# Fused attention and two MLPs on one core: phase one's small group at its end, and conversion work at other steps

## The chip, the cores and the metric

One core of one Trainium2 chip runs the whole program. The metric is device time in microseconds (us) of one execution; the median of several is compared. Nothing is shared with other cores.

## The reference

```python
I = inducing                                   # 32 x 128
h = softmax(I @ x.T / sqrt(128)) @ x           # over 12480 tokens: 32 x 128
x1 = softmax(x @ h.T / sqrt(128)) @ h          # 12480 x 128
g = max(x1 @ w_in, 0) + alpha * min(x1 @ w_in, 0)   # 12480 x 2048
x2 = g @ w_out                                 # 12480 x 128
out = max(x2 @ w2_in, 0) ** 2 @ w2_out         # 12480 x 128
```

x and inducing are fp32; the four weight matrices (128x2048 or 2048x128) and alpha come in 8-byte words, so a quarter of a weight matrix is 512 KB and is turned into fp32 on the chip.

## The kernel before, in words

All large products run in a reduced fp32 format, each operand split into a high and a low part; `three` (L688 to 691) does hi*hi, lo*hi and hi*lo into one PSUM bank. There are eight PSUM banks: h1 (two), h2 (two), y1 (one), y2 (two), ms (one). The order on every engine is the order in which the program issues the instructions; nothing is reordered.

**Phase one** (L359 to 456) reads x in groups of four sub-tiles: first a small group of 4x48 tokens, then six of 4x512. For group g the loop does `scores(g)`, the values of the group before (`values1`), running maximum and exp (`maxima`, `exps`), the transposes of the next group's x (`transpose_x`, four banks, two copies by ScalarE, two by VectorE), and the transposes of e (`transpose_e`). Between these stand the conversions of w_in and w_out (`to_f32`, L181 to 210), each with five parts: MAG and LOW on ScalarE, BITS and SIGN on VectorE, ADD on GpSimd; a w_out quarter also has REST (GpSimd), HI (ScalarE) and LO (GpSimd). MAG writes a PSUM bank where one is given, else SBUF. Behind the loop (L402 to 456) come the last group, the weights `wgt` by which the four row groups of 32 are joined, the matrix `sel`, the denominator, and hT, the result of the first attention.

**Start of the main part** (L618 to 644). The softmax of the first 512 tokens (`first_attention`), the product w1 of hT and w_in (`make_w1`, `make_first_w1s`, `copy_w1`, `low_w1`), and the DMAs on SyncE that lay w1's parts into w1s (`spread_w1s`). With w1s a tile's first layer is one matmul on its attention weights a_s.

**Main loop** (L816 to 830). 25 tiles (21 of 512 tokens, three of 448, one of 384) times 16 chunks of the hidden width give 400 items. In step s PE does `l1_a(s)` (first layer, then g1h on ScalarE and g1l on VectorE), `l2_a(s-24)`, `l1_b` of an item three to five steps back and `l2_b(s-28)`; l2_split, one step after l2_a, makes g2h on ScalarE and g2l on GpSimd. So the first steps hold 1 to 4 large matmuls and all steps from 28 on 10. Two lists hang other work on steps: `at(...)` (L783 to 804) for the second softmax (`second_attention`: tiles 1 to 4 first, whose seven parts end in 16 DMAs into a_s) and for v, and PIECES (L254 to 259), whose tuples give the steps of MAG, LOW, BITS, SIGN, ADD and split for the eight quarters of w2_in and w2_out; a quarter's buffer is freed by its ADD, and then the load of the quarter four places on is issued on SyncE's queue. Tile 1 begins with l1_a(16).

```python
at(5, second[3])
at(6, second[4])
at(9, second[5])
at(10, second[6])
```

The last tile's rows are copied, transposed and written by two engines in parallel (`last_rows`, L759 to 774).

Of the kernel before, what the change touches and what calls it, by code (L numbers as in the profile page):

```python
# [30 lines left out]
def attention_then_two_mlps(ctx: ExitStack, tc, x, inducing, w_in, w_out, alpha, w2_in, w2_out, out):  # L31
# [108 lines left out]
    def load_x(g, part=None):  # L140
        _, n, p, r = groups1[g][0]
        if g in x_t:
            t = x_t[g]
# [6 lines left out]
        k = (Q, 1, 2)[min(g, 2)]  # L150
        for a in range(0, len(groups1[g]), k) if part is None else [k * part]:
            t0, kk = groups1[g][a][0], min(k, len(groups1[g]))
            (nc.scalar if g == 1 and a % 2 else nc.sync).dma_start(
                out=t[:p, a : a + kk, :r],
                in_=x[0, t0 : t0 + kk * n, :].rearrange("(t p r) c -> p t r c", p=p, r=r),
            )
# [138 lines left out]
    def scores(g):  # L295
        b = ms_bank()
# [73 lines left out]
    idle_bank = y2_bank()  # L370
    keep_busy(1, idle_bank)
    for g in range(last):
        if g:
            run(convs[g - 1][:2])
# [13 lines left out]
        if g:
            run(convs[g - 1][3:5])
        if 1 < g and g + XBUFS - 1 <= last:  # L390
            load_x(g + XBUFS - 1)
        if 0 < g <= 4:
            load_w("w_out", g - 1)
        if g == 2:
# [7 lines left out]
    b = scores(last)  # L402
    values1(last - 1)
# [3 lines left out]
    maxima(last, b)  # L407
    exps(last, b)
# [5 lines left out]
    transpose_e(last)  # L414
# [17 lines left out]
    nc.vector.tensor_scalar(sel, same, wgt, None, op0=ALU.mult)  # L432
# [32 lines left out]
    def first_attention():  # L465
# [41 lines left out]
        def step_split():
            d = a_s[0] = new_a_s(0)[: 3 * M]
            nc.scalar.copy(d, v["b"][: 3 * M, : wide[0]])
            lo = d[M : 2 * M]  # L510
            nc.vector.tensor_tensor(lo, v["b"][M : 2 * M, : wide[0]], f32(lo), op=ALU.subtract)

        return [step_scores, step_max, step_exp, step_sum, step_back, step_split]
# [347 lines left out]
```

## Time and profile before

| | us |
|---|---|
| median of 3 runs (lowest, highest) | 962.77 (961.51, 962.86) |
| profiled execution | 961.23 |
| its span, first to last instruction | 959.4 |
| PE busy | 949.3 (99%) |
| ScalarE, VectorE, GpSimd busy | 727.4, 649.9, 536.9 |

The busy share of PE counts matmuls from issue to modelled end, and they overlap; 99% therefore hides places where the pace falls. Matmuls of 512 columns that follow one another start about 0.23 us apart. In the rows further down PE is TensorE, PEld its weight loads, ACT is ScalarE, DVE is VectorE, POOL is GpSimd, SP is SyncE, and a trailing q is an engine's issuing queue.

### The profile page before, as it was taken

The numbers are of one execution on the slowest core, as the hardware profiler recorded it, in microseconds if no ns is written. First come the engines' busy times: TensorE is split into PE (matmuls) and PEld (weight loads), VectorE is DVE, ScalarE is ACT, GpSimd is POOL, SyncE is SP. The second block draws the span as 40 slices with busy tenths as digits, with TensorE's granted clock in tenths as the row PEclk, the third lists the DMA queues.
The fourth block names the chain that finished last, engine by engine and source line by source line (L and its number), as shares of the span: only waits on it lengthen the run. The fifth ranks groups of instructions, "written<-read, shape, count | busy, mean of one in ns | idle before, by whom it ended". The sixth has DMA issues, their size and how long they took to land.

```text
span 959.4 us, 13675 instructions
## 1 busy us (share of the span) xinstructions
PE 949.3 (99%) x4560; PEld 787.6 (82%) x4560; DVE 649.9 (68%) x1013; ACT 727.4 (76%) x1333; POOL 536.9 (56%) x435
## 2 busy tenths in 40 slices
PE   9989999999999999999999999999999999999998
PEld 7667778888878888878888878888888888899997
DVE  5788767666667766667666667766666766666677
ACT  5779777777777777777777777777777777777776
POOL 2548755655555655555665555565555665555530
PEclk9999999999999999999999999999999999999999
DMA  9542000020000020000020000020000020000000
GB/s 343 163 111 82 1 12 12 9 47 12 1 12 12 3 52 12 1 12 12 1 55 12 1 12 1 12 55 1 12 12 1 12 48 1 12 12 4 8 11 19
DMA packets 64551, 29.00 MB, mean 30 GB/s; under 512 B 52208, under 2 KB 57440, under 8 KB 64480
## 3 DMA queue, kind: packets, MB, share of 16 engines
q1 hardware_dynamic: 64000, 27.52, 11.5%
q8 instruction: 36, 0.59, 0.3%
q10 hardware_dynamic: 480, 0.61, 0.2%
q14 instruction: 35, 0.29, 0.1%
HBM read 14.80 MB, written 6.39 MB: 22 GB/s over the span
## 4 chain that ended last, share of the span: by engine, by line
PE 89%; ACT 2%; DVE 1%; issue 1%; POOL 0%; POOLq 0%; DVEq 0%
PE y L691 17%; PE y L690 17%; PE y L689 17%; PE h L689 9%; PE h L690 9%; PE h L691 9%; PE h L679 8%; PE y L707 1%; PE ms L524 1%; ACT g1h L683 0%; ACT r L723 0%; DVE mag L199 0%; ACT g2h L732 0%; ACT raw L195 0%; DVE mag L205 0%
## 5 line engine op out<-in xcount | busy, mean ns | idle before, releaser
L734 POOL TENSOR_TENSOR g2l<-sq,g2h 128x512 fp32r<-128x512 f32 (+1 forms) x376 | 480.0, 1278 | 342.6 <-ACT g2h L732 331.6
L685 DVE SCALAR_TENSOR_TENSOR g1l<-h,g1h 128x512 fp32r<-128x512 f32 (+2 forms) x400 | 270.0, 677 | 230.3 <-ACT g1h L683 225.1
L683 ACT ACTIVATE g1h<-h 128x512 fp32r<-128x512 f32 (+2 forms) x400 | 234.2, 588 | 141.9 <-PE h L679 140.7
L725 DVE TENSOR_TENSOR sq<-h,r 128x512 f32<-128x512 f32 (+2 forms) x400 | 271.1, 678 | 53.9 <-ACT r L723 16.9
L723 ACT ACTIVATE r<-h 128x512 f32<-128x512 f32 (+2 forms) x400 | 235.8, 589 | 61.2 <-PE h L691 16.8
L732 ACT CAST g2h<-sq 128x512 fp32r<-128x512 f32 (+2 forms) x400 | 240.8, 602 | 2.6 <-DVE sq L725 2.6
L679 PE MATMUL h<-a_s,w1s 128*128 128x512 f32 (+3 forms) x400 | 155.0, 389 | 2.8 <-DMA a_s<-a_lo 1.4
L689 PE MATMUL h<-y1h,w2i_hi 128*128 128x512 f32 (+2 forms) x400 | 154.3, 386 | 0.3
L690 PE MATMUL y<-g2h,w2o_lo 128*128 128x512 f32 (+2 forms) x400 | 153.8, 385 | 0.0
L691 PE MATMUL h<-y1l,w2i_hi 128*128 128x512 f32 (+2 forms) x400 | 153.8, 384 | 0.0
L690 PE MATMUL h<-y1h,w2i_lo 128*128 128x512 f32 (+2 forms) x400 | 153.7, 384 | 0.0
L691 PE MATMUL y<-g2l,w2o_hi 128*128 128x512 f32 (+2 forms) x400 | 153.7, 384 | 0.0
L689 PE MATMUL y<-g2h,w2o_hi 128*128 128x512 f32 (+2 forms) x400 | 153.7, 384 | 0.0
L691 PE MATMUL y<-g1l,wo_hi 128*128 128x512 f32 (+2 forms) x400 | 153.7, 384 | 0.0
L690 PE MATMUL y<-g1h,wo_lo 128*128 128x512 f32 (+2 forms) x400 | 153.7, 384 | 0.0
L689 PE MATMUL y<-g1h,wo_hi 128*128 128x512 f32 (+2 forms) x400 | 153.7, 384 | 0.0
L679 PEld LDWEIGHTS h<-a_s,w1s 128*128 128x128 f32 (+1 forms) x400 | 75.0, 188 | 25.3 <-DVE sq L725 4.1
L689 PEld LDWEIGHTS h<-y1h,w2i_hi 128*128 128x128 f32 x400 | 75.1, 188 | 16.1 <-DVE sq L725 1.8
L690 PEld LDWEIGHTS y<-g1h,wo_lo 128*128 128x128 f32 x400 | 75.1, 188 | 14.8
L689 PEld LDWEIGHTS y<-g1h,wo_hi 128*128 128x128 f32 x400 | 75.1, 188 | 14.3
L691 PEld LDWEIGHTS y<-g2l,w2o_hi 128*128 128x128 f32 x400 | 75.1, 188 | 14.2 <-DVE g2l L734 0.3
L691 PEld LDWEIGHTS y<-g1l,wo_hi 128*128 128x128 f32 x400 | 75.1, 188 | 13.9
(156 smaller groups left out, 664.5 us busy)
## 6 DMA issues: line engine op xcount, KB each, us to landing
out_dram<-o SPq DMA_DIRECT2D x84, 64.0 KB, 2.0
xg<-in_x_dram SPq DMA_DIRECT2D x8, 512.0 KB, 9.1
raw<-in_moe_w_in_dram SPq DMA_DIRECT2D x8, 512.0 KB, 5.7
raw<-in_moe_w_out_dram SPq DMA_DIRECT2D x8, 512.0 KB, 4.6
a_s<-a_hi SPq DMA_DIRECT2D x40, 64.0 KB, 2.0
a_s<-a_lo SPq DMA_DIRECT2D x40, 64.0 KB, 2.0
x_last<-in_x_dram SPq DMA_DIRECT2D x2, 512.0 KB, 9.9
out_dram<-o SPq DMA_DIRECT2D x12, 56.0 KB, 1.9
```

Source lines behind the costliest of these rows:

```text
L524: nc.tensor.matmul(b[i * M : (i + 1) * M, :w], hT[:, :M], xT[:, first_token[t + 1] - w : first_token[t + 1]], start=True, stop=True, tile_ ...
L679: nc.tensor.matmul(b[:, :w], w1s[: a.shape[0], c * P : (c + 1) * P], a, start=True, stop=True)
L683: nc.scalar.activation(hi, b[:, :w], AF.Relu)
L685: nc.vector.scalar_tensor_tensor(lo, b[:, :w], 0.0, f32(hi), op0=ALU.max, op1=ALU.subtract)
L689: nc.tensor.matmul(b, w_hi, hi, start=start, stop=False)
L690: nc.tensor.matmul(b, w_lo, hi, start=False, stop=False)
L691: nc.tensor.matmul(b, w_hi, lo, start=False, stop=stop)
L707: nc.tensor.matmul(b, v_s[: a.shape[0]], a, start=False, stop=True)
L723: nc.scalar.activation(r, b, AF.Relu)
L725: nc.vector.tensor_tensor(sq, b, r, op=ALU.mult)
L732: nc.scalar.copy(hi, sq)
L734: (nc.vector if i >= total - LAG2 else nc.gpsimd).tensor_tensor(lo, sq, f32(hi), op=ALU.subtract)
```

## The change

Phase one starts with a wide group, and the small one comes last, its transposes in the step of the last wide group's and its scores, exp and values behind that group's. The loads are issued in another order and not interleaved in halves. The matrix sel is made by ScalarE. In the first softmax, the product, the transposes and the split go in two halves; the low part of w1s' first 512 columns too, and w1l is made by GpSimd. The last w_out quarter is converted ahead of the main loop (MAG in an h1 bank) but for HI and LO. The second softmax of tiles 1 to 4 has its exp at step 8 instead of 5, sum at 9 instead of 6, way back at 12 instead of 9, split and DMAs at 13 instead of 10; v's three parts stand at 9, 10 and 12 instead of 11, 13 and 16. The w2 quarters' steps differ, and the last has its MAG in the ms bank. l1_a uses h2 for even and h1 for odd steps up to 23 and h1 from then on, where it was the other way round up to 23. The last rows are copied in pieces of 128 columns and cut at 256 instead of 128.

```diff
-    groups1 = [[(i * n0, *FIRST1) for i in range(Q)]]
+    groups1 = []
     for a in range(Q * n0, N, Q * TILE1[0]):
         groups1.append([(a + i * TILE1[0], *TILE1) for i in range(Q)])
+    groups1.append([(i * n0, *LAST1) for i in range(Q)])
+    last = len(groups1) - 1
...
-    keep_busy(4, idle_bank)
+    keep_busy(5, idle_bank)
...
-        return to_f32("w_out", k, lambda: f, h2_bank if k == 2 else None) + [rest, high, low]
+        return to_f32("w_out", k, lambda: f, {2: h2_bank, 3: h1_bank}.get(k)) + [rest, high, low]
...
-        ("w2_in", 0, y2_bank, (12, 13, 14, 14, 14, 18)), ("w2_in", 1, y2_bank, (16, 17, 18, 18, 18, 21)),
-        ("w2_out", 0, ms_bank, (19, 20, 21, 21, 21, 24)), ("w2_in", 2, ms_bank, (23, 23, 24, 24, 24, 27)),
-        ("w2_out", 1, y1_bank, (25, 25, 26, 26, 26, 29)), ("w2_in", 3, ms_bank, (27, 28, 28, 28, 28, 31)),
-        ("w2_out", 2, y1_bank, (30, 30, 31, 31, 31, 34)), ("w2_out", 3, None, (33, 33, 34, 34, 34, 38)),
+        ("w2_in", 0, y2_bank, (8, 9, 10, 11, 11, 15)), ("w2_in", 1, y2_bank, (15, 16, 17, 18, 18, 21)),
+        ("w2_out", 0, ms_bank, (19, 20, 21, 22, 22, 25)), ("w2_in", 2, ms_bank, (23, 24, 24, 25, 25, 28)),
+        ("w2_out", 1, y1_bank, (25, 26, 26, 27, 27, 30)), ("w2_in", 3, ms_bank, (27, 28, 28, 29, 29, 32)),
+        ("w2_out", 2, y1_bank, (29, 30, 30, 31, 31, 34)), ("w2_out", 3, ms_bank, (31, 32, 32, 33, 33, 36)),
...
+    nc.scalar.dma_start(out=ind, in_=inducing)
     load_x(0)
+    load_w("w_in", 0)
     load_x(1)
-    load_x(2, 0)
-    load_w("w_in", 0)
-    load_x(2, 1)
-    load_x(3, 0)
     load_w("w_in", 1)
-    load_x(3, 1)
+    load_x(2)
     nc.sync.dma_start(out=al_raw, in_=alpha.rearrange("(c p) -> c p", p=P))
+    load_w("w_in", 2)
+    load_x(3)
+    load_w("w_in", 3)
     load_x(4)
-    load_w("w_in", 2)
-    load_x(5)
-    load_w("w_in", 3)
+    load_x(last)
...
         run(transpose_x(g + 1))
+        if g == last - 2:
+            run(transpose_x(last))
         transpose_e(g)
...
-    nc.vector.tensor_scalar(sel, same, wgt, None, op0=ALU.mult)
+    nc.scalar.mul(sel, same, wgt)
+    values1(last - 1)
     values1(last)
...
     convs[6][SIGN]()
+    convs[7][BITS]()
     convs[5][REST]()
...
     def low_w1():
-        nc.vector.tensor_tensor(w1["lo"], w1["bank"], f32(w1["hi"]), op=ALU.subtract)
+        pool_lo(w1["lo"], w1["f"], w1["hi"])
...
     copy_w1()
     first[3]()
+    run(mult)
     low_w1()
-    first[4]()
-    first_w1s_low()
-    first[5]()
+    run(back)
+    run(high)
+    first_w1s_low(0, 256)
+    run(low)
+    first_w1s_low(256, 512)
+    convs[7][SIGN]()
+    convs[7][ADD]()
     step_wa()
     convs[5][HI]()
     convs[6][HI]()
+    convs[7][REST]()
...
     spread_w1s("lo", 3)
+    load_w(*PIECES[3][:2])
     convs[5][LO]()
...
-        b = h2_bank() if other_bank else h1_bank()
+        b = h1_bank() if other_bank else h2_bank()
...
-        cut = w // P // 2 * P
+        cut = w - P
...
-    at(5, second[3])
-    at(5, convs[7][BITS])
-    at(6, second[4])
-    at(7, convs[7][SIGN])
-    at(7, convs[7][ADD])
-    at(7, load_w, *PIECES[3][:2])
-    at(9, second[5])
-    at(10, second[6])
-    at(10, convs[7][REST])
-    at(11, step_v)
-    at(13, copy_v)
-    at(13, convs[7][HI])
-    at(13, convs[7][LO])
-    at(16, split_v)
+    at(6, convs[7][HI])
+    at(6, convs[7][LO])
+    at(8, second[3])
+    at(9, second[4])
+    at(9, step_v)
+    at(10, copy_v)
+    at(12, second[5])
+    at(12, split_v)
+    at(13, second[6])
...
-            l1_a(s, s < LAG2 and s % 2)
+            l1_a(s, s >= LAG2 or s % 2)
```

## Rows read from the trace of the kernel before

**Rows 1.** Busy time by stretches: stretch; then us busy and instructions of each engine
```profile
200.00:900.00 700.00, 700.00 (x3137) 582.68 (x3136) 460.99 (x684) 532.60 (x953) 403.77 (x317) 1.00 0.07 14
```

**Rows 2.** Timeline, PE, first transposes: start, us from start to end, engine, line
```profile
5.75 3.65 PE L286 MATMUL h<-ident,xg 128*128 128x128 f32 x16
...
11.40 1.97 PE L286 MATMUL h<-ident,xg 128*128 128x128 f32 x16
```

**Rows 3.** DMA issues by line: count, size, median us to landing
```profile
xg<-in_x_dram SPq DMA_DIRECT2D x2, 256.0 KB, 4.8
```

**Rows 4.** Timeline, PE and ScalarE, last group's transposes of x and e
```profile
31.25 0.64 PE L339 MATMUL y<-ident,e 128*128 128x128 f32 x4
...
31.45 0.59 ACT L289 COPY xT<-h 128x512 f32<-128x512 f32 x1 [0.35 <-PE h L286]
```

**Rows 5.** Timeline: the small group's exp, and the end of phase one
```profile
5.76 0.30 ACT L323 ACTIVATE e<-ms,nm 128x48 f32<-128x48 f32 x1 [1.64 <-DVE nm L318]
...
37.25 1.29 POOL L208 TENSOR_TENSOR w_out_sb<-mag,raw 128x512 int32<-128x512 int32 x1 [2.08 <-ACT raw L195]
37.27 1.35 DVE L432 TENSOR_SCALAR sel<-same,wgt 128x128 f32<-128x128 f32 x1
...
39.80 0.29 DVE L448 TENSOR_TENSOR hT<-y,den 128x128 f32<-128x128 f32 x1
```

**Rows 6.** Timeline, DVE and PE, from the first softmax to the first l1_a
```profile
43.03 0.56 DVE L495 TENSOR_TENSOR a<-y,mx 128x384 f32<-128x384 f32 x1
...
43.51 0.68 DVE L598 TENSOR_TENSOR w1l<-h,w1h 128x512 fp32r<-128x512 f32 x1
...
45.00 0.68 DVE L511 TENSOR_TENSOR a_s<-y,a_s 32x512 fp32r<-32x512 f32 x1
...
45.74 1.19 PE L679 MATMUL h<-a_s,w1s 96*128 96x512 f32 x4
```

**Rows 7.** DVE, groups from 46.85 to 57.3 us, and its last row there
```profile
L685 DVE SCALAR_TENSOR_TENSOR g1l<-h,g1h 128x512 fp32r<-128x512 f32 x10 | 6.5, 672 | 1.2 <-ACT g1h L683 1.2
L205 DVE SCALAR_TENSOR_TENSOR mag<-raw,mag 128x512 int32<-128x512 int32 x1 | 1.3, 1278 | 0.0
...
57.26 0.69 DVE L554 STREAM_TRANSPOSE a2t<-a 128x512 f32<-128x512 f32 x1
```

**Rows 8.** Timeline, SyncE's queue and PE up to l1_a(16); the wait's busy times
```profile
57.54 0.34 SPq L178 DMA_DIRECT2D raw<-in_moe_w_in_dram  x1
...
61.20 0.58 SPq L565 DMA_DIRECT2D a_s<-a_lo  x1
...
63.33 0.47 PE L679 MATMUL h<-a_s,w1s 128*128 128x512 f32 x1 [1.41 <-DMA a_s<-a_lo]
...
61.90:63.30 1.40, 0.03 (x1) 0.00 (x0) 0.59 (x1) 1.27 (x3) 1.09 (x1) 1.00 0.50 117
```

**Rows 9.** Timeline, POOL, first and last of 19 operations from 75.77 to 100.71
```profile
75.77 1.29 POOL L213 TENSOR_TENSOR w2o_lo<-wf,w2o_hi 128x512 fp32r<-128x512 f32 x1 [1.44 <-ACT w2o_hi L247]
...
99.39 1.32 POOL L213 TENSOR_TENSOR w2o_lo<-wf,w2o_hi 128x512 fp32r<-128x512 f32 x1
```

**Rows 10.** Timeline, DVE and PE, the last w2 quarter's BITS and PE behind it
```profile
98.20 2.79 DVE L199 TENSOR_SCALAR mag<-mag 128x512 int32<-128x512 int32 x1
...
100.77 0.50 PE L690 MATMUL y<-g2h,w2o_lo 128*128 128x512 f32 x1
...
102.97 0.50 PE L689 MATMUL h<-y1h,w2i_hi 128*128 128x512 f32 x1
```

**Rows 11.** Timeline of the tail; then the granted clock (third from right) behind it
```profile
955.00 0.27 ACT L765 COPY o<-y 128x128 f32<-128x128 f32 x1 [1.12 <-PE y L691]
...
955.32 0.90 PE L769 MATMUL h<-ident,o 128*128 128x128 f32 x3 [0.36 <-ACT o L765]
...
956.25 0.42 DVE L771 COPY r<-h 128x256 f32<-128x256 f32 x1 [0.53 <-PE h L769]
...
958.40:959.40 1.00, 0.00 (x0) 0.00 (x0) 0.00 (x0) 0.00 (x0) 0.00 (x0) 0.50 0.00 0
```

More of the change, by code (lines that the diff above doesn't have):

```diff
@@ L149, in load_x @@
             t = st.tile([n, Q, r, C], F32, name="x0", tag="x0")
[L150 to L155, printed above, removed]
-            )
-            if g == 0:
-                nc.scalar.dma_start(out=ind, in_=inducing)
+        k = Q if g == last else 2 if g else 1
+        for a in range(0, Q, k) if part is None else [k * part]:
+            t0 = groups1[g][a][0]
+            (nc.scalar if g == 0 and a % 2 else nc.sync).dma_start(
+                out=t[:p, a : a + k, :r],
+                in_=x[0, t0 : t0 + k * n, :].rearrange("(t p r) c -> p t r c", p=p, r=r),
+            )
         x_t[g] = t
@@ L293, in transpose_x, with scores @@
         return evac
-    def scores(g):
-        b = ms_bank()
+    def scores(g, bank=ms_bank):
+        b = bank()
         for i, (t0, n, _, _) in enumerate(groups1[g]):
@@ L305, in attention_then_two_mlps @@
     nm, e, f, s_g, eT, hb = {}, {}, {}, {}, {}, {}
-    last = len(groups1) - 1
     def small(name):
-        return att.tile([P, 1], F32, name=name, tag=name, bufs=2)
+        return att.tile([P, 1], F32, name=name, tag=name, bufs=3 if name == "f" else 2)
     def maxima(g, b):
@@ L332, in sums, with transpose_e @@
             nc.vector.tensor_copy(s_run, s_g[g])
-    def transpose_e(g):
+    def transpose_e(g, bank=y1_bank):
         _, _, p, r = groups1[g][0]
-        b = y1_bank()
+        b = bank()
         own = e[g].rearrange("n (p r) -> n r p", r=r)
@@ L369, in attention_then_two_mlps @@
     nc.vector.tensor_copy(indT, b[:, :M])
[L370 to L374, printed above, removed]
+    run(transpose_x(0))
+    for g in range(last - 1):
+        run(convs[g][:2])
         b = scores(g)
@@ L383, in attention_then_two_mlps @@
             add_values(g - 1)
-            convs[g - 1][2]()
+        convs[g][2]()
         run(transpose_x(g + 1))
+        if g == last - 2:
+            run(transpose_x(last))
         transpose_e(g)
         sums(g)
[L388 to L394, printed above, removed]
+        run(convs[g][3:5])
+        if g == 1:
+            load_x(XBUFS)
+        if g < 4:
+            load_w("w_out", g)
+        if g == 1:
             b = y2_bank()
@@ L400, in attention_then_two_mlps @@
     MAG, LOW, BITS, SIGN, ADD, REST, HI, LO = range(8)
-    b = scores(last)
-    values1(last - 1)
+    b, bs = scores(last - 1), scores(last, h1_bank)
+    values1(last - 2)
     convs[4][REST]()
@@ L406, in attention_then_two_mlps @@
     convs[6][MAG]()
-    maxima(last, b)
-    exps(last, b)
+    maxima(last - 1, b)
+    maxima(last, bs)
+    exps(last - 1, b)
+    exps(last, bs)
     b = y2_bank()
@@ L413, in attention_then_two_mlps @@
     convs[4][HI]()
-    transpose_e(last)
+    transpose_e(last - 1)
+    transpose_e(last, h2_bank)
     m_all = att.tile([1, M], F32, name="m_all", tag="m_all")
@@ L421, in attention_then_two_mlps @@
     keep_busy(2, idle_bank)
-    add_values(last - 1)
+    add_values(last - 2)
+    sums(last - 1)
     sums(last)
-    nnm = att.tile([P, 73 + M], F32, name="nnm", tag="nnm")[:, :1]
+    nnm = att.tile([P, 65 + M], F32, name="nnm", tag="nnm")[:, :1]
     nc.vector.tensor_scalar_mul(nnm, nm[last], -1.0)
@@ L437, in attention_then_two_mlps @@
     run(convs[7][:2])
+    add_values(last - 1)
     d = ms_bank()
@@ L493, in step_sum, with halves, mult, back @@
             nc.vector.reciprocal(r, sm)
-            w = v["a"] = att.tile([P, nb, 3, M], F32, name="a1", tag="a2")
+            v["a"] = att.tile([P, nb, 3, M], F32, name="a1", tag="a2")
+            v["b"] = y1_bank()
+            v["d"] = a_s[0] = new_a_s(0)[: 3 * M]
+        def halves(f):
+            k = nb // 2
+            return [lambda: f(0, k), lambda: f(k, nb)]
+        def mult(i, e):
             nc.vector.tensor_tensor(
-                w, a.unsqueeze(2).to_broadcast([P, nb, 3, M]),
-                r.unsqueeze(2).unsqueeze(3).to_broadcast([P, nb, 3, M]), op=ALU.mult,
-            )
-        def step_back():
-            b = v["b"] = y1_bank()
-            for i in range(nb):
+                v["a"][:, i:e], block(v["s"])[:, i:e].unsqueeze(2).to_broadcast([P, e - i, 3, M]),
+                v["r"][:, i:e].unsqueeze(2).unsqueeze(3).to_broadcast([P, e - i, 3, M]), op=ALU.mult,
+            )
+        def back(i, e):
+            for k in range(i, e):
                 nc.tensor.transpose(
-                    b[: 3 * M, i * P : (i + 1) * P], v["a"][:, i].rearrange("p r j -> p (r j)"), ident
+                    v["b"][: 3 * M, k * P : (k + 1) * P], v["a"][:, k].rearrange("p r j -> p (r j)"), ident
                 )
[L507 to L513, printed above, removed]
+        def high(i, e):
+            nc.scalar.copy(v["d"][:, i * P : e * P], v["b"][: 3 * M, i * P : e * P])
+        def low(i, e):
+            lo = v["d"][M : 2 * M, i * P : e * P]
+            nc.vector.tensor_tensor(lo, v["b"][M : 2 * M, i * P : e * P], f32(lo), op=ALU.subtract)
+        return [step_scores, step_max, step_exp, step_sum], halves(mult), halves(back), halves(high), halves(low)
     def second_attention(tiles):
@@ L584, in make_w1, with first_w1s_low @@
             )
-    def first_w1s_low():
-        nc.vector.tensor_tensor(w1s[64:, :512], w1["first"][64:], f32(w1s[64:, :512]), op=ALU.subtract)
+    def first_w1s_low(a, e):
+        nc.vector.tensor_tensor(w1s[64:, a:e], w1["first"][64:, a:e], f32(w1s[64:, a:e]), op=ALU.subtract)
     def copy_w1():
@@ L616, in scale_wa @@
         )
-    first = first_attention()
+    first, mult, back, high, low = first_attention()
     second = second_attention(groups[0])
@@ L623, in attention_then_two_mlps @@
     make_first_w1s()
-    keep_busy(2, y2_bank(), same)
+    keep_busy(1, y2_bank(), same)
     run(first[1:3])
@@ L760, in last_rows @@
         w = wide[NT - 1]
-        cut = w // P // 2 * P
-        parts = ((nc.scalar.copy, nc.scalar, 0, cut), (nc.vector.tensor_copy, nc.sync, cut, w))
+        cut = w - P
         rows = out[first_token[NT - 1] :, :].rearrange("(k p) c -> p k c", p=P)
-        for copy, _, a, e in parts:
-            copy(o[:, a:e], b[:, a:e])
-        for copy, queue, a, e in parts:
+        for k in range(0, w, P):
+            (nc.scalar.copy if k < cut else nc.vector.tensor_copy)(o[:, k : k + P], b[:, k : k + P])
+        for copy, queue, a, e in ((nc.scalar.copy, nc.scalar, 0, cut), (nc.vector.tensor_copy, nc.sync, cut, w)):
             d = h1_bank()
```

12 lines of the change are left out of this document (4 added, 8 removed).

## The prediction, made before the changed kernel ran

> **What bounds the kernel now.** I first read the busy table by stretches [rows 1]: from 200 to 900 us TensorE (PE) is busy all the time, and the diff touches nothing that repeats there. So a time can only come from the stretch before PE is full (about 0 to 103 us) and from the last 5 us; what is won or lost there reaches the end one to one, because the work behind it is the same. Then I read the timeline of that stretch, engine by engine, from phase one [rows 2 to 5] to the start of the main loop [rows 6], its first tile [rows 7, 8], the steps where w2 is converted [rows 9, 10], and the tail [rows 11]. The reader should see five places where PE does not set the pace: the first transposes, the end of phase one, the way back of the first softmax, tile 1's wait, and the convoy on GpSimd (POOL) around 100 us.
>
> The profiled execution took 961.23 us (span 959.4 and 1.8 around it); the median of the runs shown is 962.77, 1.54 more, so I add the sum to that median. About 0.2% (1.9 us) is what a measurement of this kernel can tell from no change.
>
> **The change, part by part.** Minus is earlier.
>
> *Start, -1.3.* Today the first wide group's transposes begin at 5.75 and their 16 take 3.65 us where the next group's take 1.97 [rows 2]: the 1.2 GHz level against 2.4. Ahead of them stand the small group's load and its whole chain. Now the wide load is issued first, at 0.74 instead of 1.18, with no 96 KB before it. A 256 KB piece lands 4.8 us after issue today [rows 3]; 0.44 earlier and without its forerunner I take 4.4 to 5.0 for the first piece, so transposes end near 8.2 and the second group's begin near 10.1 instead of 11.40. Bounds: 0, if the second group's load or the half clock holds it back; -1.75, if neither does. The six wide groups follow at the old pace, since each still moves 1 MB of x and 0.5 MB of weights.
>
> *Last group's transposes in the step before, +0.95.* The 48-column transposes reuse the four banks that the wide group's transposes have just filled. The last waits until ScalarE's copy ends at 31.45 + 0.59 = 32.04, so the transposes of e, which started at 31.25, start at about 32.2 [rows 4]. Bounds +0.3 (PE's four small transposes alone) and +1.0.
>
> *End of phase one, about 0.* From the last wide scores on, ScalarE has a second exp with its two short followers and a second, small copy of eT ahead of wgt; from the 0.30 that the small exp takes today [rows 5] I put the four at 0.9. sel today waits on DVE for GpSimd's add, 37.25 to 38.54, and takes 1.35 us; a 128x128 copy on ScalarE takes 0.27 [rows 5, 11], so -1.0. But then h_run's last sums (two now) end last, behind the values' matmuls; hT comes at 39.8 + 0.95 - 0.05, less the start's 1.3: 39.4. Bounds -0.5, +0.6 (recip, which reads SBUF, meeting the add).
>
> *Way back in halves and w1l, -0.7.* Between hT and the first main matmul DVE today does the product 0.56, w1l 0.68, w1s' low part and a_s' low part 0.68 in turn [rows 6]. w1l goes to GpSimd, where it costs the 1.3 of such a subtraction [rows 9]; only half of w1s' low part stays ahead, and ScalarE's copy starts half a product earlier. First l1_a: 44.6 instead of 45.74, all told -1.1. w1l is then ready only at about 45.1 (GpSimd's adds run till 43.9), so SyncE's spread of it lands near 47.8 and holds l1_a(4), which DVE would not take before 50: nothing. If DVE were not behind, 1 us. Bounds -0.4 to -0.8.
>
> *Bank swap, +0.4.* l1_a(1) now gets the h1 bank that holds convs[7]'s magnitude; SIGN (0.69) is behind w1s' second half on DVE, so l1_a(1) comes 1 us after l1_a(0), and DVE, which follows ScalarE, loses 0.4 (0 to 0.7).
>
> *Second softmax three steps later, +1.5.* From its first g1l, 1.16 us behind the first l1_a, DVE works without a pause; today 10.4 us pass before the way back at 57.26: ten g1l at 0.60 pitch, the softmax, and convs[7]'s BITS and SIGN, the second of 1.28 [rows 7]. Then a_hi, a_lo, tile 1's second low piece issued at 61.20, and l1_a(16), which it lets go, at 63.33 [rows 8]: 6.1 us. Now thirteen g1l (7.8), four operations of the softmax and of wa (2.9) and the first w2 piece's BITS and SIGN (0.6 each) come first: 11.9 us. SyncE is also passed: the w2 load of step 7 moves ahead of the loop, but another 512 KB load is issued at step 12, just before a_s' DMAs. Today's, at 57.54, is as near to them [rows 8]; I take nothing, at most +0.5. step_v, two steps earlier, no longer waits for w_out's last part, but PE waits anyway. a_s is there at about 64.2, while PE, with nothing else to do, stands from 60.0: a wait of 4.2 us where it was 1.4. Range +0.8 to +2.
>
> *split_v at step 12, -0.35:* its matmul and wait leave the steps after 16.
>
> *w2 pieces, -0.55.* From 75.77 to 100.71 GpSimd does 19 operations of about 1.3 (1.25 in pitch) nearly without a gap, and PE's matmul on w2o_lo at 100.77 follows the last [rows 9, 10]. Then DVE's BITS of the last piece, with its magnitude in SBUF, takes 2.79 behind GpSimd, and PE, which could go on at 101.4, stands until 102.97: 1.55 [rows 10]. In a PSUM bank that is a 0.69 operation. But the last piece's ADD is now one step earlier, ahead of that w2o_lo: one more operation, +1.25, in the convoy, less some 0.3 that its start gains. -1.55 + 0.95 = -0.6, say -0.55; bounds -1.5 (no wait on w2o_lo) and +0.8 (all of it, and the earlier pieces too).
>
> *Tail, -0.3.* DVE's branch, two copies of 256 columns at 0.42, ends last, at 956.67 [rows 11]; it gets 128 columns (0.27 on ScalarE) and ScalarE 256. Bounds 0, -0.4.
>
> Sum: -1.1 + 0.4 + 1.5 - 0.35 - 0.55 - 0.3 = **-0.4 us**, so 962.4: gains ahead of the loop that the later second softmax gives back.
>
> **Rivals.**
>
> *PE's clock falls in tile 1's wait (slower).* For: the wait grows to some 4 us, and the trace shows the granted clock at 0.50 at 958.4, 2.2 us after the last matmul [rows 11]; today's wait, 61.9 to 63.33, keeps 1.00 [rows 8]. Against: the wait may be shorter if DVE is less late than I add up. [...] Price: the one half-speed stretch that the trace has, the first 16 transposes, cost 3.65 - 1.97 = 1.7 us [rows 2]; once to twice that on top of -0.4 gives +1.3 to +3.0, in the middle 964.9. The Trainium skill, page "TensorE: Matmul & The Clock Gate", section "HAM oscillation — how this bites in real kernels", says that a wait between bursts of matmuls that is long enough puts the array back to half rate and that the next burst then starts cold. By that rule this rival would hold; no wait in the loop of before is long enough to show it.
>
> *The front's gain arrives (faster).* If DVE is not the bound in steps 5 to 12, the a_s DMAs land as early as today's relative to the loop's start, and the second softmax costs nothing; and if GpSimd hides its extra add, the 1.55 of 100.8 to 103 goes whole. -1.1 + 0.4 - 0.35 - 1.55 - 0.3 = -2.9: 959.9. For: DVE is rid of convs[7]'s BITS and SIGN (1.28) in just these steps [rows 7]. Against: DVE's queue is in order and without a gap [rows 7], and GpSimd's convoy is full [rows 9].
>
> *The start gains nothing.* If PE is slow until the second group's transposes as well, the start is worth 0: -0.4 + 1.3 = +0.9, 963.7, still within 0.2%.
>
> **How the numbers follow.** Forecast 0.43, clock 0.27, front 0.26, start 0.04. The forecast's own unknowns, about 1.1 us, leave a twentieth of it on either side of 0.2%; of the clock rival three quarters are slower by over 0.2%, of the front rival nearly all is faster. Together: faster 0.28, same 0.48, slower 0.24. The range, 959.2 to 965.4, reaches from the front's case to the clock's upper middle; the forecast's own is 961 to 963.8.
>
> **What would show it.** Right: second group's transposes near 10.1; hT near 39.4; sel on ScalarE at 0.3 us; first l1_a near 44.6; l1_a(16) near 64.2 after a wait of about 4 us on a_s<-a_lo; no DVE operation of 2.8 us at 98, but a wait on w2o_lo of about a microsecond. Matmuls at 0.43 us spacing behind l1_a(16) show the clock rival; l1_a(16) before 62.5 shows the front rival. A first l1_a later than 45.7, or a wait elsewhere in the loop of over 1.5 us, makes the sum wrong.

## The result, and the profile after

The changed kernel takes 968.15 us (median of 6 runs, 966.00 to 972.34) where the kernel before takes 961.48 (6 runs beside them, 961.05 to 962.86): ratio 1.0070, 95% interval 1.0049 to 1.0091. It is slower, by more than the forecast's range allowed (959.2 to 965.4). The profiled execution is the fastest of the six, 966.00 us with a span of 964.2, against 961.23 and 959.4 before: 4.8 us more. The longer ones have a lower mean granted clock: 0.998 at 966.00 us, 0.996 at 967.84, 0.995 at 968.89, 0.989 at 972.34.

The start of some l1_a items cuts the two spans into stretches that can be compared. "T1" is the start of the second group's x transposes; a stretch's length is the difference of two landmarks.

| stretch | before | after | difference | forecast |
|---|---|---|---|---|
| 0 to T1 | 11.40 | 10.72 | -0.68 | -1.3 |
| T1 to hT | 28.41 | 30.54 | +2.13 | +0.9 |
| hT to l1_a(16) | 23.53 | 25.74 | +2.21 | +1.2 |
| l1_a(16) to (24) | 7.86 | 9.24 | +1.38 | -0.35 |
| l1_a(24) to (40) | 38.46 | 38.32 | -0.14 | -0.55 |
| l1_a(40) to (399) | 812.19 | 812.19 | 0.00 | 0 |
| l1_a(399) to the end | 37.6 | 37.5 | -0.1 | -0.3 |

The sum is +4.8. The steady loop is unchanged to the last digit; all but the tail's 0.1 lies in the first 115 us. Each fence below, where no other view is named, is the timeline of the changed kernel (start, us, engine, line, operation, and in brackets the idle time ahead and what ended it), and answers to a group of rows of before.

TensorE at the start, which answers to [rows 2]:

```profile
3.87 1.12 PE L283 MATMUL h<-ident,xg 128*128 128x128 f32 x4
5.45 1.97 PE L283 MATMUL h<-ident,xg 128*128 128x128 f32 x8 [0.46 <-DMA xg<-in_x_dram]
7.95 1.12 PE L283 MATMUL h<-ident,xg 128*128 128x128 f32 x4 [0.54 <-DMA xg<-in_x_dram]
...
10.72 1.97 PE L283 MATMUL h<-ident,xg 128*128 128x128 f32 x16
```

The first group now begins at 3.87 instead of 5.75, but its pieces come one by one, and PE stands between them.

The end of phase one, on TensorE, VectorE, GpSimd and ScalarE in turn, which answers to [rows 4, 5]:

```profile
31.76 0.75 PE L335 MATMUL y<-ident,e 128*128 128x128 f32 x4
...
36.54 0.27 PE L403 MATMUL y<-ident,nm 128*1 128x128 f32 x1 [2.07 <-DVE nm L312]
...
34.30 0.92 DVE L312 SCALAR_TENSOR_TENSOR nm<-top,nm 128x1 f32<-128x1 f32 x1
35.14 0.19 DVE L310 TENSOR_REDUCE top<-h 128x1 f32<-128x48 f32 x1
36.33 0.16 DVE L312 SCALAR_TENSOR_TENSOR nm<-top,nm 128x1 f32<-128x1 f32 x1 [0.99 <-ACT f L322]
...
41.26 0.29 DVE L445 TENSOR_TENSOR hT<-y,den 128x128 f32<-128x128 f32 x1
...
34.16 1.04 POOL L223 TENSOR_TENSOR aw<-w_out_sb,al 128x512 f32<-128x512 f32 x1
...
36.01 0.28 ACT L322 ACTIVATE f<-nm 128x1 f32<-128x1 f32 x1
...
38.70 0.40 ACT L427 ACTIVATE sel<-same,wgt 128x128 f32<-128x128 f32 x1
```

PE waits 2.07 us for the running maximum nm of the small group. Two things make it late. The nm of the wide group takes 0.92 us, while the same operation takes 0.16 for the small one; GpSimd's 1.04 us multiplication runs beside it, and both end at 35.2. And the small group's nm starts only at 36.33, 1 us behind its top: nm has two buffers, and ScalarE's f at 36.01 still reads the one to be written.

The way back of the first softmax, on VectorE and then TensorE, which answers to [rows 6]:

```profile
44.49 0.62 DVE L501 TENSOR_TENSOR a<-y,mx 128x192 f32<-128x192 f32 x2
45.42 0.43 DVE L593 TENSOR_TENSOR w1s<-h,w1s 64x256 fp32r<-64x256 f32 x1 [0.31 <-ACT w1s L600]
46.30 0.75 DVE L517 TENSOR_TENSOR a_s<-y,a_s 32x256 fp32r<-32x256 f32 x2 [0.45 <-ACT a_s L513]
47.09 0.43 DVE L593 TENSOR_TENSOR w1s<-h,w1s 64x256 fp32r<-64x256 f32 x1
47.55 0.69 DVE L205 SCALAR_TENSOR_TENSOR mag<-raw,h 128x512 int32<-128x512 int32 x1
...
47.20 1.59 PE L692 MATMUL h<-a_s,w1s 96*128 96x512 f32 x4 [0.17 <-DVE a_s L517]
```

The first l1_a comes 5.94 us behind hT, as before (45.74 - 39.80), although w1l's 0.68 is gone from VectorE: it now stands idle for 0.31 and 0.45 us, waiting for ScalarE. The low halves start when ScalarE has made both high halves, so the two halves overlap little.

Tile 1's start, on VectorE, SyncE's queue and TensorE, which answers to [rows 8]:

```profile
60.68 0.70 DVE L560 STREAM_TRANSPOSE a2t<-a 128x512 f32<-128x512 f32 x1
...
62.12 0.51 SPq L571 DMA_DIRECT2D a_s<-a_hi  x1
63.42 0.51 SPq L571 DMA_DIRECT2D a_s<-a_lo  x1
...
64.62 0.58 SPq L571 DMA_DIRECT2D a_s<-a_lo  x1
...
67.00 0.77 PE L692 MATMUL h<-a_s,w1s 128*128 128x512 f32 x1 [4.55 <-DMA a_s<-a_lo]
67.56 0.63 PE L702 MATMUL y<-g1h,wo_hi 128*128 128x512 f32 x1
67.99 0.63 PE L703 MATMUL y<-g1h,wo_lo 128*128 128x512 f32 x1
```

The a_lo issued at 64.62 is tile 1's second low piece, which l1_a(16) waits for; before it was issued at 61.20 [rows 8].

The busy times of stretches around it, and of the steady loop [rows 1] (us; then busy us and instructions of PE, PEld, DVE, ACT and POOL; the granted clock is third from the right):

```profile
62.50:67.00 4.50, 0.00 (x0) 0.03 (x1) 1.29 (x2) 1.56 (x4) 2.16 (x2) 1.00 0.69 189
67.00:70.40 3.40, 3.40 (x8) 2.75 (x9) 0.95 (x2) 1.76 (x3) 0.00 (x0) 0.50 0.43 103
70.40:75.00 4.60, 4.60 (x21) 3.75 (x21) 4.30 (x7) 3.54 (x7) 1.33 (x1) 1.00 0.34 81
200.00:900.00 700.00, 700.00 (x3134) 582.24 (x3133) 461.03 (x683) 532.18 (x952) 403.18 (x316) 1.00 0.08 15
```

PE does nothing from 62.5 on, and when it begins again the granted clock is 0.50, the 1.2 GHz level, for 3.4 us: the matmuls behind l1_a(16) come 0.43 us apart instead of 0.23.

The convoy on GpSimd (its operations one right behind the other), on TensorE and then GpSimd, which answers to [rows 9, 10]:

```profile
95.33 0.39 PE L702 MATMUL y<-g2h,w2o_hi 128*128 128x512 f32 x1
97.11 0.50 PE L703 MATMUL y<-g2h,w2o_lo 128*128 128x512 f32 x1 [1.39 <-POOL w2o_lo L213]
...
94.49 1.33 POOL L747 TENSOR_TENSOR g2l<-sq,g2h 128x512 fp32r<-128x512 f32 x1
95.76 1.30 POOL L213 TENSOR_TENSOR w2o_lo<-wf,w2o_hi 128x512 fp32r<-128x512 f32 x1
```

The VectorE operation of 2.79 us is gone, but step 32 waits for w2o_lo: 1.78 us from one matmul to the next instead of 0.23. In step 36, where the forecast looked for this wait, it is 0.87, and 0.28 before. The tail's copies are shorter as planned ([rows 11]: 0.42), and give 0.1:

```profile
961.15 0.29 DVE L783 COPY r<-h 128x128 f32<-128x128 f32 x1 [0.42 <-PE h L781]
...
960.82 0.37 ACT L783 COPY r<-h 128x256 f32<-128x256 f32 x1 [0.42 <-PE h L781]
```

### The profile page after: what moved, and what is told of

The parts are those of the page before. It is cut to its first block, busy times and chain, and to the rows that moved or that the text cites. A ratio compares the mean times of both kernels' runs of the same rounds, so it can differ in the third digit from the quotient of the medians.

```text
span 964.2 us, 13671 instructions
## 1 busy us (share of the span) xinstructions
PE 949.2 (98%) x4556; PEld 787.2 (82%) x4556; DVE 646.7 (67%) x1014; ACT 729.2 (76%) x1336; POOL 537.8 (56%) x436
## 4 chain that ended last, share of the span: by engine, by line
PE 95%; ACT 2%; DMA 1%; DVE 1%; issue 0%; POOL 0%; SPq 0%; ACTq 0%; DVEq 0%; POOLq 0%
PE y L703 18%; PE y L704 18%; PE y L702 18%; PE h L692 9%; PE h L702 9%; PE h L703 9%; PE h L704 9%; PE h L283 1%; PE ms L295 1%; DMA xg<-in_x_dram 1%; PE y L720 1%; PE y L344 1%; PE ms L530 1%; ACT g1h L696 0%; PE y L335 0%
## 5 line engine op out<-in xcount | busy, mean ns | idle before, releaser
L703 PEld LDWEIGHTS y<-g2h,w2o_lo 128*128 128x128 f32 x400 | 75.1, 188 | 15.6 <-POOL w2o_lo L213 2.7
```

The costliest lines, as they stand in the source:

```text
L703: nc.tensor.matmul(b, w_lo, hi, start=False, stop=False)
```

## The experiments

Names with e and f are edits of the changed kernel, names with b of the kernel before. The ratio is to the kernel before, run beside them; it is formed over all the runs and is not exactly the ratio of the two medians.

| run | us, median (range) | ratio (95% interval) |
|---|---|---|
| e1 | 965.28 (963.86 to 967.12) | 1.0044 (1.0029 to 1.0059) |
| e2 | 966.31 (965.89 to 969.59) | 1.0061 (1.0045 to 1.0077) |
| e3 | 965.94 (965.32 to 966.35) | 1.0049 (1.0034 to 1.0064) |
| e4 | 967.21 (963.01 to 970.61) | 1.0057 (1.0035 to 1.0079) |
| f1 | 963.73 (962.44 to 964.27) | 1.0008 (0.9996 to 1.0019) |
| f2 | 961.12 (960.49 to 962.15) | 0.9994 (0.9985 to 1.0003) |
| f3 | 960.68 (960.19 to 961.88) | 0.9993 (0.9984 to 1.0001) |
| f4 | 960.26 (959.14 to 960.84) | 0.9984 (0.9975 to 0.9992) |
| f5 | 959.25 (958.55 to 961.48) | 0.9976 (0.9968 to 0.9984) |
| b1 | 964.31 (963.61 to 966.02) | 1.0025 (1.0014 to 1.0037) |
| b2 | 960.32 (960.00 to 961.12) | 0.9985 (0.9976 to 0.9995) |
| b3 | 959.77 (959.43 to 962.76) | 0.9985 (0.9973 to 0.9996) |
| b4 | 958.60 (958.44 to 958.89) | 0.9967 (0.9955 to 0.9979) |

Since the clock at the start shifts a whole profile, parts are compared by stretches between landmarks, as in the table above.

**e1: the second softmax back at its old steps.**

```diff
-    at(8, second[3])
-    at(9, second[4])
+    at(5, second[3])
+    at(6, second[4])
...
-    at(12, second[5])
-    at(13, second[6])
+    at(9, second[5])
+    at(10, second[6])
```

> The changed kernel with the second softmax's exp, sum, way back and split at steps 5, 6, 9 and 10 again, nothing else. Theory W (the wait for tile 1's a_s and the clock that falls in it make the loss): l1_a(16) comes 2 to 3 us earlier than 67.0, the granted clock stays at 1.00 or the low stretch is shorter, and the median falls by 3 to 5 us from 968.2. Theory P (phase one's longer end and GpSimd's convoy make it; the wait would be made up later): less than 1 us. Against W stands that exp at step 5 must wait for GpSimd's subtraction, which ended at 54.2 in the changed kernel: then a wait of about 2 us appears before l1_a(10), and W gains only 1 to 2 us.

hT to l1_a(16) was 24.09 us instead of 25.74: the later steps cost 1.65. The half-speed stretch stayed (66.97 to 70.38): PE still waits 1.98 us there, now for VectorE's g1l and no longer for a_s, and l1_a(16) to (24) took 9.24. The median fell by 2.9, a little less than theory W said, though its clock did not hold.

```profile
66.31 0.47 PE L692 MATMUL h<-a_s,w1s 128*128 128x512 f32 x1 [1.98 <-DVE g1l L698]
```

**e2: fill matmuls in tile 1's wait.** They multiply constants into a bank that is not read; each of the 15 has two rows in the trace (x30).

```diff
     at(13, second[6])
+    at(15, lambda: keep_busy(15, y2_bank(), same))
```

> The changed kernel with 15 idle matmuls on PE at step 15, inside its wait for tile 1 (about 4 us of work for a wait of 4.6). The wait's end stays at 67.0. Theory W: the granted clock stays at 1.00 there, matmuls behind l1_a(16) follow at 0.23 us instead of 0.43, l1_a(18) comes 1.4 us earlier, the median falls by 2 to 4 us from 968.2 and the runs lie within 1 us of one another. Theory P: the clock's share is the profiled run's 1.4 us at most, and the spread of 6 us between the runs stays.

The timeline of TensorE, and the busy times behind l1_a(16):

```profile
63.72 3.51 PE L98 MATMUL y<-same 128*128 128x128 f32 x30
68.58 0.47 PE L692 MATMUL h<-a_s,w1s 128*128 128x512 f32 x1 [1.35 <-DMA a_s<-a_lo]
```

```profile
68.60:72.00 3.40, 3.40 (x15) 2.81 (x16) 1.88 (x3) 2.33 (x5) 0.00 (x0) 1.00 0.46 111
```

The data come no sooner, but the clock is 1.00 behind them and 15 matmuls run in the 3.4 us in which 8 ran. l1_a(16) to (24) falls from 9.24 to 7.63: this one stretch costs 1.6. The run as a whole is still slow: here the clock came up only at 13.19 in the start. The median fell by 1.8, and the runs lie 3.7 us apart, not within 1 us: this wait alone is not the spread.

**e3: three buffers for nm.**

```diff
-        return att.tile([P, 1], F32, name=name, tag=name, bufs=3 if name == "f" else 2)
+        return att.tile([P, 1], F32, name=name, tag=name, bufs=3 if name in ("f", "nm") else 2)
...
-    nnm = att.tile([P, 65 + M], F32, name="nnm", tag="nnm")[:, :1]
+    nnm = att.tile([P, 57 + M], F32, name="nnm", tag="nnm")[:, :1]
```

> The changed kernel with three buffers for nm (and 32 bytes less of the unused tail of another tile, so that nothing else moves). The small group's nm no longer waits until ScalarE has read the one from two groups back: nm at about 35.4 instead of 36.33, hT about 0.9 us earlier, near 40.3. Theory P: the time falls by 0.9 us or more. Theory W: it falls by 0.9 us too unless the clock's low stretches change, which can hide it (plus or minus 2 us).

Both nm operations on VectorE:

```profile
34.43 0.92 DVE L312 SCALAR_TENSOR_TENSOR nm<-top,nm 128x1 f32<-128x1 f32 x1
...
35.50 0.16 DVE L312 SCALAR_TENSOR_TENSOR nm<-top,nm 128x1 f32<-128x1 f32 x1
```

The second follows the first at once. T1 to hT fell from 30.54 to 29.71: the missing buffer cost 0.83. The half-speed stretch at tile 1 was twice as long in this profile (65.10 to 71.93), and l1_a(16) to (24) took 10.22.

**e4: quarters three to eight of w2 at before's steps**, the last still with MAG in the ms bank.

```diff
-        ("w2_out", 0, ms_bank, (19, 20, 21, 22, 22, 25)), ("w2_in", 2, ms_bank, (23, 24, 24, 25, 25, 28)),
-        ("w2_out", 1, y1_bank, (25, 26, 26, 27, 27, 30)), ("w2_in", 3, ms_bank, (27, 28, 28, 29, 29, 32)),
-        ("w2_out", 2, y1_bank, (29, 30, 30, 31, 31, 34)), ("w2_out", 3, ms_bank, (31, 32, 32, 33, 33, 36)),
+        ("w2_out", 0, ms_bank, (19, 20, 21, 21, 21, 24)), ("w2_in", 2, ms_bank, (23, 23, 24, 24, 24, 27)),
+        ("w2_out", 1, y1_bank, (25, 25, 26, 26, 26, 29)), ("w2_in", 3, ms_bank, (27, 28, 28, 28, 28, 31)),
+        ("w2_out", 2, y1_bank, (30, 30, 31, 31, 31, 34)), ("w2_out", 3, ms_bank, (33, 33, 34, 34, 34, 38)),
```

> The changed kernel with quarters 3 to 8 of w2 at the steps of before (the last still in the ms bank). Both theories: GpSimd's adds no longer stand ahead of the low part that step 32 needs, and the wait of 1.78 us there goes, as does that at step 36; l1_a(37) comes 1 to 1.7 us earlier relative to l1_a(24). Theory P gives the whole of it in the time; theory W gives it too, plus or minus what the clock's low stretches do.

The wait in step 32 is gone, and none takes its place (in step 36 it is 0.26):

```profile
99.36 0.39 PE L702 MATMUL y<-g2h,w2o_hi 128*128 128x512 f32 x1
99.59 0.39 PE L703 MATMUL y<-g2h,w2o_lo 128*128 128x512 f32 x1
```

l1_a(24) to (40) took 36.56 instead of 38.32, 1.8 less. The total hardly shows it: this profile has a half-speed stretch from 40.09 to 43.51 as well, T1 to hT took 32.0, and the runs spread over 7.6 us.

**f1: the clock held.** e2 and e3 together, and fill matmuls between the first group's transposes and ahead of nm's transpose.

```diff
+    start_bank = y2_bank()
     run(transpose_x(0))
...
+            if g == 0 and i in (0, 2):
+                keep_busy(1 + i // 2, start_bank)
...
+    idle_bank = h1_bank()
+    keep_busy(3, idle_bank)
     b = y2_bank()
     nc.tensor.transpose(b[:1, :P], nm[last], ident)
```

> The changed kernel with three buffers for nm, and with idle matmuls on PE in its three waits: one and two between the first group's transposes, three ahead of the transpose of nm at the end of phase one, fifteen ahead of l1_a(16). No useful work moves. Theory C (the changed kernel's extra time beyond hT's chain and tile 1's wait, and the spread of 6 us between its runs, are the clock's low stretches): the granted clock rises once, near 9 us, and stays at 1.00; hT near 40.4, l1_a(16) 25.7 us behind it, and the runs lie within 1 us of one another at about 963.6. If the spread has another cause, the runs still lie 3 us apart and the median stays at 965 or above.

The clock rose at 6.36 and stayed up to the end of the work. The median is where theory C put it; the range shrank from 6.3 us to 1.8, not to 1, and what is left comes at a mean granted clock of 0.999 or 1.000 in every run, so it is not the clock. The ratio fell from 1.0070 to 1.0008. Less the nm buffer's 0.83, the clock's share is 3.6 us by the medians (968.15 - 963.73 - 0.83) and 5.1 by the ratios (0.0062 of 961 is 6.0). The two differ because the runs of before beside f1 spread more (960.89 to 964.60): 10 of the 31 have a mean granted clock of 0.996 or 0.997 and take 962.60 or more, and the medians alone would give 1.0025.

**b1: the second softmax at the new steps in the kernel before**, and nothing else of the change.

```diff
-    at(5, second[3])
-    at(6, second[4])
-    at(9, second[5])
-    at(10, second[6])
+    at(8, second[3])
+    at(9, second[4])
+    at(12, second[5])
+    at(13, second[6])
```

> The kernel before with the second softmax's exp, sum, way back and split at steps 8, 9, 12 and 13, nothing else. Theory W: the a_s of tile 1 comes 2 to 3 us later, PE waits about 4 us at l1_a(16), the granted clock falls to 0.50 there for 3.4 us or longer, and the time is 3 to 5 us above before. Rival: GpSimd's and DVE's other work of the change makes the wait, not the steps; then l1_a(16) moves by under 1 us and the time by under 1 us.

TensorE at tile 1, and the busy times there:

```profile
64.44 0.77 PE L679 MATMUL h<-a_s,w1s 128*128 128x512 f32 x1 [3.97 <-DMA a_s<-a_lo]
65.01 0.63 PE L689 MATMUL y<-g1h,wo_hi 128*128 128x512 f32 x1
```

```profile
63.00:69.80 6.80, 5.36 (x14) 4.33 (x15) 2.87 (x6) 3.20 (x7) 1.28 (x1) 0.50 0.44 103
```

This one move is enough to lose the clock: hT to l1_a(16) took 1.17 longer than before, and l1_a(16) to (24) 10.38 instead of 7.86, another 2.5. Of this, 0.6 comes back in l1_a(24) to (40), 37.88 instead of 38.46.

**b2: sel by ScalarE, in the kernel before.**

```diff
-    nc.vector.tensor_scalar(sel, same, wgt, None, op0=ALU.mult)
+    nc.scalar.mul(sel, same, wgt)
```

> The kernel before with sel made by ScalarE, nothing else. sel takes about 0.4 us and no longer waits for GpSimd's add (1.35 us); h_run's last sum starts at 37.8 instead of 38.54 and hT comes 0.7 us earlier. Prediction's view: -0.7 us in the time, if the clock and tile 1's wait stay as they are. Rival: h_run's sum meets something else on DVE, or tile 1's wait takes it up: 0.

```profile
36.50 0.40 ACT L432 ACTIVATE sel<-same,wgt 128x128 f32<-128x128 f32 x1
```

0.40 us where VectorE's took 1.35 beside GpSimd's add [rows 5]; hT at 38.64, T1 to hT 27.34 instead of 28.41.

**b3: the last quarter's MAG in the ms bank, in the kernel before.**

```diff
-("w2_out", 3, None, (33, 33, 34, 34, 34, 38)),
+("w2_out", 3, ms_bank, (33, 33, 34, 34, 34, 38)),
```

> The kernel before with the last w2 quarter's magnitude in the ms bank, nothing else. Prediction's view: BITS takes 0.7 us instead of 2.8, PE's loss of 1.55 us between 101 and 103 goes and the time falls by 1.5 us. Rival: GpSimd's full queue makes another wait there, and less than 0.5 us comes out.

l1_a(24) to (40) took 36.95 instead of 38.46: the 1.5 us behind the 2.79 us operation are gone.

**b4: b2 and b3 together.**

> The kernel before with the two of the change's edits that each saved time alone: sel on ScalarE, and the last w2 quarter's MAG in the ms bank. My theory: the two places lie apart (hT, and steps 33 to 37) and nothing absorbs the first gain before the second, so they add: ratio 0.998 and 0.998 give 0.997, about 958.7 us; hT near 38.6, l1_a(24) near 70.0, l1_a(40) minus l1_a(24) near 37.0. Rival: GpSimd's convoy is fixed in time by loads rather than by the steps, so an earlier start is lost in it: l1_a(40) minus l1_a(24) near 38, ratio 0.998 to 0.999.

VectorE's BITS and SIGN of the last quarter:

```profile
96.84 0.69 DVE L199 TENSOR_SCALAR ms<-ms 128x512 int32<-128x512 int32 x1
97.57 0.69 DVE L205 SCALAR_TENSOR_TENSOR mag<-raw,ms 128x512 int32<-128x512 int32 x1
```

The two add up: T1 to hT 27.33, l1_a(24) to (40) 36.99. At 958.60 us this is the fastest kernel of the study, 0.33% ahead of before and 9.5 us ahead of the changed one.

**f2: f1 with e4's steps for the w2 pieces.**

> The changed kernel with the clock held up (fill matmuls) and three nm buffers, and with the w2 pieces at the steps of before but the last MAG in the ms bank. My theory: the wait on w2o_lo in step 32 goes without a new one: l1_a(40) minus l1_a(24) 36.6 instead of 38.4, 1.8 us earlier than the same kernel with the change's steps (ratio 1.001): ratio 0.999, about 961.9. Rival: with the clock up the convoy's cover is other and the wait comes back in another step: the difference stays over 38 and the ratio at 1.001.

l1_a(24) to (40) took 36.58 instead of f1's 38.37, and the ratio came to 0.9994: as expected.

**f3: f2 with e1's steps for the second softmax.**

> As the run before it, and the second softmax's parts back at steps 5, 6, 9, 10. My theory: l1_a(16) minus hT 24.1 instead of 25.8, so another 1.5 to 1.7 us: ratio 0.997 to 0.998, about 960.3; with all three places mended the changed kernel is then no slower than before. Rival: the way back is set by DVE's queue whatever its step, l1_a(16) minus hT stays at 25.5 or more and the ratio at 0.999.

A miss: hT to l1_a(16) fell only to 25.20, not to 24.1. TensorE there:

```profile
62.74 3.51 PE L98 MATMUL y<-same 128*128 128x128 f32 x30
66.00 0.48 PE L696 MATMUL h<-a_s,w1s 128*128 128x512 f32 x1
```

l1_a(16) has no wait in its row: the fill itself, sized for the longer wait, held it back.

**f4: f3 with 7 fill calls instead of 15.**

```diff
-    at(15, lambda: keep_busy(15, y2_bank(), same))
+    at(15, lambda: keep_busy(7, y2_bank(), same))
```

> The run before this one (clock held, three nm buffers, before's steps for the w2 pieces and for the second softmax) with 7 fill matmuls at step 15 instead of 15. There l1_a(16) stood directly behind the fill, at hT + 25.2, although a_s' second low piece had been issued at 61.58. My theory: the fill itself was the bound; l1_a(16) comes at hT + 24.1 and waits again on a_s<-a_lo, the clock still holds, 1.1 us earlier: ratio 0.998, about 959.6 us. Rival: the data were no earlier, l1_a(16) stays at hT + 25 or more behind a wait, and the ratio at 0.999.

```profile
62.85 1.72 PE L98 MATMUL y<-same 128*128 128x128 f32 x14
65.00 0.47 PE L696 MATMUL h<-a_s,w1s 128*128 128x512 f32 x1 [0.44 <-DVE g1l L702]
...
63.04 1.89 DVE L702 SCALAR_TENSOR_TENSOR g1l<-h,g1h 128x512 fp32r<-128x512 f32 x3
```

hT to l1_a(16) is 24.13, and the clock held: f3's miss was the fill. What ends the wait is not a_s, as expected, but g1l on VectorE (63.04 + 1.89 = 64.93), whose result frees the bank. The median gained 0.4 of the 1.1 us. With all of this the changed kernel is 0.16% faster than before.

**f5: f4 without a GpSimd operation beside nm.** REST (GpSimd, the multiplication `aw` of the fence above), HI (ScalarE) and LO (GpSimd) of the first w_out quarter move behind the next quarter's ADD, out of the stretch.

```diff
-    convs[4][REST]()
...
-    convs[4][HI]()
...
     convs[5][ADD]()
+    convs[4][REST]()
...
     run(convs[7][:2])
+    convs[4][HI]()
...
-    convs[4][LO]()
...
     low_w1()
+    convs[4][LO]()
```

> As the kernel with the shorter fill, and convs[4]'s REST (GpSimd), HI and LO moved behind convs[5]'s ADD, out of the stretch in which nm is made. My theory: the small VectorE operation on nm takes 0.16 instead of 0.92 us because no GpSimd operation runs beside it, and hT comes 0.7 us sooner behind the second group's transposes (29.0 instead of 29.7), a little more if ScalarE's eT copy, now without HI ahead of it, was on the path: ratio 0.997. Rival: nm stays at 0.9 (the delay has another source), or nm falls and the values' matmuls or ScalarE's exp end last, so that hT stays at 29.5 or later.

```profile
36.20 0.16 DVE L314 SCALAR_TENSOR_TENSOR nm<-top,nm 128x1 f32<-128x1 f32 x1
...
36.51 0.16 DVE L314 SCALAR_TENSOR_TENSOR nm<-top,nm 128x1 f32<-128x1 f32 x1
```

nm takes 0.16, and T1 to hT 29.17 instead of 29.73, 0.56 of the 0.7 expected; the median fell by 1.0. In this profile the clock fell even so, in the start:

```profile
9.10:12.40 3.30, 3.30 (x12) 1.07 (x12) 0.00 (x0) 1.72 (x3) 0.00 (x0) 0.50 1.04 407
```

## Why the prediction was wrong

The forecast was no change; the kernel is slower, and the rival with a chance of 0.27, the clock's fall in tile 1's wait, holds in its mechanism, though not in its price: it said +1.3 to +3.0, and the medians differ by 6.7. The forecast's base, 962.77, was also 1.3 above the 961.48 of six runs; from that base its -0.4 gives 961.1. Against the sum, 5.2 us are missing in the profiled execution (+4.8 for -0.4), 1.7 of them in l1_a(16) to (24), 1.2 in T1 to hT, 1.0 in hT to l1_a(16), 0.6 in the start. Step by step:

- **The clock.** The step that failed is the choice against this rival. The forecast itself had a wait of 4.2 us there (4.55 measured) and still priced its clock at nothing, on the ground that the wait might be shorter. Fill in the wait (e2) and the move alone (b1) show the cause: with PE idle the clock behind it is 0.50, with PE filled it is 1.00. The price was said as once to twice 1.7; here it is 1.6 (9.24 against e2's 7.63), in e3 2.6 (10.22 against 7.63) and in b1 2.5 (10.38 against 7.86 before). What the rival left out is that the clock also falls elsewhere in some runs: in e4 it reads 0.50 from 40.09 to 43.51, behind a wait of 2.08 us for nm that ended at 38.36, and in f5 from 9.05 to 12.47, in a wait of 2.17 us for x that ended at 9.08, although f5 has f1's fill in the start. f1 has fill in all three places and puts the clock's share at 3.6 to 5.1 us, and most of the spread of 6.3 us goes with it; what each of the other two places costs was not tested alone. The Trainium skill, page "TensorE: Matmul & The Clock Gate", section "HAM oscillation — how this bites in real kernels", has this as a wait between bursts after which the next burst starts cold; the trace agrees (0.50 from 67.00 to 70.41).
- **Start, -1.3.** The sum had its pieces land together. They land one by one, and T1 is 0.68 earlier in this profile; in the five profiles without fill in the start (after, e1 to e4) it lies between 10.72 and 12.54, in the five of before's between 10.88 and 11.40. Not all of that is the clock: in f2 and f3 it was up by 5.8, and T1 is still 10.64 and 11.08, behind waits of 1.46 and 1.78 us for the last piece. So there is no gain to rely on: the rival "the start gains nothing" holds as well, beside the clock.
- **Last group's transposes, +0.95.** Near, a little over its bound of +1.0: e's transposes stand 21.04 us behind T1 (31.76 - 10.72) instead of 19.85, +1.2 with the gaps.
- **End of phase one, about 0.** sel on ScalarE is right in size (-1.0 said, -1.07 by b2). But the sum had only durations and no buffers: the wide and the small group now make nm in immediate succession, which costs 0.83 for the two buffers (e3), and 0.56 for the GpSimd operation beside nm (f5, which also moves ScalarE's HI). Together 1.4, against 1.2 by which T1 to hT exceeds the forecast.
- **Way back in halves and w1l, -0.7.** Wrong: 0.0. The step took VectorE's queue for the path; the trace of after has idle time on VectorE there, ended by ScalarE. No run undid the halves alone, so that cause is read from the trace and not tested.
- **Bank swap, +0.4.** Not there: l1_a(1) comes 0.37 behind l1_a(0), not 1 us (0.34 before). l1_a(0) to (8) takes 6.14 instead of 5.93 in this profile, but 5.91 to 5.93 in e2, e3 and e4, whose first eight steps are the same; the 0.2 comes between l1_a(7) and l1_a(8), and its cause is open.
- **Second softmax, +1.5.** Right: 1.65 by e1, 1.17 by b1 in the kernel before. Undoing it does not bring before's 23.53 back (24.09 in e1): VectorE's queue, with the first w2 quarter's BITS and SIGN now in these steps, ends last there, as the g1l in e1's and f4's row says; that these two operations make it late was not tested.
- **w2 pieces, -0.55.** Of its two terms the first is right (-1.55 said, -1.5 by b3); the convoy's, +0.95, is mis-sized: 1.8 by e4 and f2. Step 36, where the sum had it, waits 0.6 longer; the other 1.55 is step 32, which only the bound of +0.8 ("the earlier pieces too") had in view. The stretch as a whole came to -0.14.
- **Tail, -0.3, and split_v, -0.35.** -0.1, and about -0.2 (l1_a(16) to (24) 7.63 in e2, 7.86 before).

Mending the places one by one (f1 to f5) brings the changed kernel from 1.0070 to 0.9976. What it keeps above b4 lies mostly in T1 to hT (29.17 against 27.33) and hT to l1_a(16) (24.13 in f4 against 23.60).

## What to carry to other kernels

Where an edit makes TensorE wait some microseconds longer, its price can be the wait and slower matmuls behind it. If the wait can't go, small matmuls on constants in it held the clock here (e2, f4); more of them than the wait is long cost 1.1 us (f3 against f4). Before two instances of a stage are put back to back, count the buffers of its small tiles and what GpSimd runs beside them. And test the edits of a large change one at a time: two single lines of this one gave 0.33%, and the rest of it cost 1.0% (0.70 + 0.33).

## What was not expected of the hardware

In after the granted clock reads 1.00 throughout the idle 4.5 us, and 0.50 only from where the matmuls return. Elsewhere it falls at another place: in b1, e3 and e4 1.4, 1.3 and 2.9 us before they return, in e1 0.7 us behind. e3's stretch before l1_a(16), as busy times:

```profile
65.10:66.38 1.28, 0.00 (x1) 0.03 (x1) 0.00 (x0) 0.00 (x0) 0.00 (x0) 0.50 0.46 109
```

The half-speed stretch at tile 1 was 3.4 us long in after and e1, and 6.8 in e3, e4 and b1; what costs time is the part of it that falls on matmuls (3.4 us cost 1.6 in after, 5.55 cost 2.6 in e3). With seven fill matmuls (14 rows, 1.72 us) in a wait of 2.2 us the clock stayed at 1.00 (f4); e1, with a wait of 1.98 us and no fill, lost it.

A VectorE operation on 128x1 elements takes 0.16 us alone and 0.92 beside GpSimd's multiplication of 128x512, in all nine profiles in which it starts 0.13 or 0.14 us behind it, and ends with it; in before, where it starts 0.23 ahead of it and has ended when it starts, and in f5, where that multiplication is moved away, it takes 0.16 or 0.17. The Trainium skill, page "SBUF — State Buffer", section "SBUF: two separate sides", says that a VectorE operation with two inputs in SBUF and a GpSimd operation that reads SBUF share a port pair, and that the one that starts first holds it to its end. The trace agrees, with the multiplication first: 34.16 + 1.04 = 35.20, and 34.30 + 0.92 = 35.22.
